# An attention kernel fused with an MLP: a different mask for the first chunks, ScalarE copies, reordered loads, one more crossbar transpose and a split last output block

## The chip, the cores and the metric

The kernel runs on one core of one Trainium2 chip. The metric is device time in microseconds (us) of one execution, lower is better. The span that a profile shows is some 1.8 us shorter than the time of the same execution (218.6 against 220.45 us for the kernel before).

TensorE does the matmuls (PE in the profile, PEld its weight loads), VectorE (DVE) and ScalarE (ACT) the elementwise work, GpSimd (POOL) some elementwise work and the issuing of the loads, SyncE (SP) the issuing of the stores and of the transposing DMAs.

## The reference, cut to what matters

Lightning attention (linear attention with a decay per head) feeds an MLP with an ELU.

```python
# q, k, v: [B=4, H=8, S=768, D=64]; lam: [8]; w_in: [512, 2048]; w_out: [2048, 512]
for b in range(nb):                      # blocks of 64 rows; the kernel uses chunks of 128
    intra = (qb @ kb.T) * Dmask          # Dmask[i, j] = lam ** (i - j) for i >= j, else 0
    intra = intra @ vb
    inter = (qb * lam_pow) @ kv_state    # lam_pow[i] = lam ** (i + 1)
    out[:, :, sl] = intra + inter
    kv_state = lam ** block * kv_state + (kb * rev_pow).T @ vb
x = out.transpose(0, 2, 1, 3).reshape(B * S, H * D)    # 3072 tokens x 512
h = x @ w_in
g = where(h > 0, h, exp(min(h, 0)) - 1)
return g @ w_out
```

## The kernel before

A chunk is 128 rows of one batch element with all eight heads; there are 24, numbered g = 4c + b (c is the place in the sequence, b the batch element). Chunks 0 to 3 have no state behind them. Four chunks make a token block of the MLP, so there are six blocks. Block 0's first matmul (h = x @ w_in, 16 steps of 128 columns) is called phase A here, and its second (g @ w_out) phase B. From block 1 on the two matmuls of neighbouring blocks are interleaved, and attention chunks are woven in between. A pair of chunks has a "visit" of three parts: transposes and the decayed keys `kd`; scores `psS` and their mask; then output `psO`, state update `psU` and the copy into the MLP's input `xt`.

The decay lam^(i−j) is factored: the mask holds only the part of j (with the causal zeros), and the part of i is multiplied in by VectorE when `psO` goes to `xt`.

```python
LOADS = [(0,1,'q'), (0,1,'k'), (0,1,'v'), ..., (3,1,'k'), ('wi',0), (2,1,'v'), ('wi',1), (3,1,'v'),
         ('wi',2), ('wi',3), ('wi',4), ('wi',5), ('kd',0), ('wi',6), ('kd',2), ('wo',0), (4,2), ...]
# every load is issued by POOL in this order; ('kd', g) is a multiply on POOL between the issues

nc.scalar.activation(dn[:], loglam[:], AF.Exp, scale=pos[:, 0:1])
for hh in range(2):                                   # the mask of all chunks, once, on VectorE
    nc.vector.tensor_tensor(out=mask[:, hh], in0=causT..., in1=dn..., op=ALU.mult)
zero_states(nc.vector)                                # four memsets
# ... (cut)
def att_X(g, n, parts=1):                             # psO -> xt, with the part of i
    nc.vector.tensor_tensor(out=xt[t][...], in0=po[...], in1=qs[...], op=ALU.mult)
# ... (cut)
def mm1(t, n, alt=False):                             # one step of the first MLP matmul
    ...
    nc.scalar.activation(e[:], pH[:], AF.Exp)
    if alt:                                           # steps 3, 5, 7 of block 0: VectorE does the rest
        return e, None, pH
    nc.scalar.activation(r[:], pH[:], AF.Relu)
    return e, r, pH

def elu(t, n, e, r, pH):                              # g = min(e - 1, r): two inputs in SBUF
    nc.vector.scalar_tensor_tensor(out=gt[t][:, n, :], in0=e[:], scalar=-1.0, in1=r[:],
                                   op0=ALU.add, op1=ALU.min)
# ... (cut)  mm2, the last output block:
    nc.vector.tensor_copy(o[:, 0:hw], pm[:, 0:hw]);  nc.sync.dma_start(...)
    nc.scalar.copy(o[:, hw:], pm[:, hw:]);           nc.scalar.dma_start(...)
# ... (cut)  the start: warm-up matmuls between the parts, W[i] of them each
W = [5, 2, 3, 0, 1, 0, 0, 1, 1, 0, 0]
# ... (cut)  pairs whose q and k are transposed by a DMA, and the step that issues it
XT = {12: (1, 10), 14: (2, 2), 16: (2, 10), 18: (3, 2), 20: (3, 10), 22: (4, 2)}
visits: 4 at A11, A13, A15;  6 at B6, B9, B12;  8 at (1,0), (1,2), (1,5);  10 at (1,8), (1,10), (1,13) ...
```

Of the kernel before, what the change touches and what calls it, by code (L numbers as in the profile page):

```python
# [15 lines left out]
def kernel(  # L16
# [93 lines left out]
        [cpool.tile([128, 2, HP, 128], FP16, name=f"st{j}_{i}") for i in range(2)]  # L110
        for j in range(B // 2)
    ]
    def zero_states(e):
        for j in range(B // 2):
            for i in range(2):
                e.memset(st[j][i][:], 0.0)

    LOADS = [(0, 1, 'q'), (0, 1, 'k'), (0, 1, 'v'), (1, 1, 'q'), (1, 1, 'k'), (1, 1, 'v'), (2, 1, 'q'), (2, 1, 'k'), (3, 1, 'q'), (3, 1, 'k'), ('wi', 0), (2, 1, 'v'), ('wi', 1), (3, 1, 'v'), ('wi', 2), ('wi', 3), ('wi', 4), ('wi', 5), ('kd', 0), ('wi', 6), ('kd', 2), ('wo', 0), (4, 2), ('wo', 1), (6, 2), ('wo', 2), ('wo', 3), (8, 2), (10, 2), (12, 2), (14, 2), (16, 2), (18, 2), (20, 2), (22, 2)]

    def run_loads(items):  # L120
        for it in items:
# [18 lines left out]
    ident16 = cpool.tile([128, 128], FP16, name="ident16")  # L140
    causT = cpool.tile([128, 128], FP32, name="causT")
    rel = cpool.tile([128, 128], FP32, name="rel")
    nc.vector.tensor_copy(rel[:], rel_i[:])
    nc.vector.tensor_copy(pos[:, 0:1], rel[:, 0:1])
    nc.vector.tensor_scalar(
        out=ident16[:], in0=rel[:], scalar1=0.0, scalar2=None, op0=ALU.is_equal
    )
    nc.vector.tensor_scalar_add(pos[:, 1:2], pos[:, 0:1], float(L))
    nc.vector.tensor_scalar(
        out=causT[:], in0=rel[:], scalar1=0.0, scalar2=None, op0=ALU.is_ge  # L150
    )
    nc.vector.tensor_scalar(
        out=row[:], in0=rel[:], scalar1=pos[:, 0:1], scalar2=None, op0=ALU.subtract
    )

    dn = cpool.tile([128, H], FP32, name="dn")
    nc.scalar.activation(dn[:], loglam[:], AF.Exp, scale=pos[:, 0:1])
    mask = cpool.tile([128, 2, HP, 128], FP32, name="mask")
    for hh in range(2):
        nc.vector.tensor_tensor(  # L160
            out=mask[:, hh],
            in0=causT[:].unsqueeze(1).broadcast_to([128, HP, 128]),
            in1=dn[:, hh::2].unsqueeze(2).broadcast_to([128, HP, 128]),
            op=ALU.mult,
        )

    zero_states(nc.vector)
    ks = cpool.tile([128, H], FP32, name="ks")
    up_p = cpool.tile([128, HP], FP32, name="up_p")
    qs = cpool.tile([128, HP, 128], FP32, name="qs")  # L170
    loglam_p = cpool.tile([128, HP], FP32, name="loglam_p")

    def late_consts():
        for hh in range(2):
            r = slice(hh * 64, (hh + 1) * 64)
            nc.scalar.copy(loglam_p[r, :], loglam[r, hh::2])
        for hp in range(HP):
            nc.scalar.activation(
                qs[:, hp, :], row[:], AF.Exp, scale=loglam_p[:, hp : hp + 1]
            )  # L180
        nc.scalar.activation(ks[:], loglam[:], AF.Exp, scale=pos[:, 1:2])
        nc.scalar.activation(up_p[:], loglam_p[:], AF.Exp, scale=float(L))



# [72 lines left out]
    def att_mask(g, parts=1):  # L258
        P = asb.tile([128, 2, HP, 128], FP16, tag="P", name=f"P{g}", bufs=3)
        s = pS.pop(g)  # L260
        w = HP // parts
        for i in range(parts):
            c = slice(i * w, (i + 1) * w)
            nc.vector.tensor_tensor(  # L264
                out=P[:, :, c], in0=s[:, :, c], in1=mask[:, :, c], op=ALU.mult
            )
        Pt[g] = P

# [24 lines left out]
    def att_X(g, n, parts=1):  # L293
        t, i = where[g]
        if i == 0:
            xt[t] = asb.tile([128, HP, TS[t] * L], FP16, tag="xt", name=f"xt{t}")
        po = pS.pop(("O", g))
        w = HP // parts
        for j in range(parts):
            c = slice(j * w, (j + 1) * w)  # L300
            nc.vector.tensor_tensor(  # L301
                out=xt[t][:, c, i * L : (i + n) * L].rearrange("p h (n l) -> p n h l", n=n),
                in0=po[:, :, c],
                in1=qs[:, c].unsqueeze(1).broadcast_to([128, n, w, 128]),
                op=ALU.mult,
            )
# [68 lines left out]
            )  # L375

    def mm1(t, n, alt=False):
        MT = TS[t] * L
        if (t, n) not in pH_of:
            mm1_mm(t, n, 0, MT, "M" if t == 0 and n % 2 == 1 and n < 8 else "H")  # L380
        pH = pH_of.pop((t, n))
        e = msb.tile([128, MT], FP32, tag="e", bufs=3, name=f"e{t}_{n}")
        nc.scalar.activation(e[:], pH[:], AF.Exp)  # L383
        if alt:
            return e, None, pH
        r = msb.tile([128, MT], FP16, tag="r", bufs=3, name=f"r{t}_{n}")
        nc.scalar.activation(r[:], pH[:], AF.Relu)  # L387
        return e, r, pH

    def elu(t, n, e, r, pH):  # L390
        if r is None:
            m = msb.tile([128, TS[t] * L], FP16, tag="r", bufs=3, name=f"m{t}_{n}")
            nc.vector.tensor_scalar(
                out=m[:], in0=e[:], scalar1=-1.0, scalar2=0.0, op0=ALU.add, op1=ALU.min
            )
            nc.vector.tensor_tensor(out=gt[t][:, n, :], in0=m[:], in1=pH[:], op=ALU.max)  # L396
            return
        nc.vector.scalar_tensor_tensor(  # L398
            out=gt[t][:, n, :], in0=e[:], scalar=-1.0, in1=r[:], op0=ALU.add, op1=ALU.min
        )  # L400

    def mm2(t, i, n, tag="M"):
        if n == 0:
            psM[t, i] = ps.tile([128, DM], FP32, tag=tag, bufs=2, name=f"psM{t}_{i}")
        pm = psM[t, i]
        nc.tensor.matmul(  # L406
            pm[:], lhsT=gt[t][:, n, i * L : (i + 1) * L],
            rhs=wo_t[wo_at[n][0]][:, wo_at[n][1], :], start=(n == 0), stop=(n == NF - 1),
        )
        if n < NF - 1:  # L410
            return
        c, b = divmod(T0[t] + i, B)
        t0 = b * S + c * L
        o = msb.tile([128, DM], FP32, tag="osb", bufs=3, name=f"osb{t}_{i}")
        last = T0[t] + i == NG - 1
        if last:
            hw = DM // 2
            nc.vector.tensor_copy(o[:, 0:hw], pm[:, 0:hw])
            nc.sync.dma_start(out=out[t0 : t0 + L, 0:hw], in_=o[:, 0:hw])
            nc.scalar.copy(o[:, hw:], pm[:, hw:])  # L420
            nc.scalar.dma_start(out=out[t0 : t0 + L, hw:], in_=o[:, hw:])
        else:
            if i % 2:
                nc.vector.tensor_copy(o[:], pm[:])  # L424
            else:
                nc.scalar.copy(o[:], pm[:])  # L426
            nc.sync.dma_start(out=out[t0 : t0 + L, :], in_=o[:])
        psM.pop((t, i))
# [23 lines left out]
    def op_T(c, w):  # L452
        att_T(c, 1, w, "H")

    def op_Te(c, w):
        att_Te(c, 1, w, "a")

    W = [5, 2, 3, 0, 1, 0, 0, 1, 1, 0, 0]
    warm(W[0])
    op_T(0, "q")  # L460
    op_Te(0, "q")
    warm(W[1])
    op_T(0, "k")
    op_Te(0, "k")
    late_consts()
    warm(W[2])
    att_S(0)
    att_mask(0, 2)
# [6 lines left out]
    att_O(0, 1, "M")  # L475
    att_X(0, 1)
    warm(W[5])
    op_T(2, "q")
    op_Te(2, "q")
    att_S(1)  # L480
    att_mask(1, 2)
    warm(W[6])
    op_T(2, "k")
    op_Te(2, "k")
    op_T(3, "q")
    op_Te(3, "q")
    warm(W[7])
    att_S(2)
    att_mask(2, 2)
    op_T(3, "k")  # L490
    op_Te(3, "k")
    att_O(1, 1, "M")
    att_X(1, 1)
    warm(W[8])
    att_S(3)
    att_O(2, 1, "M")
    att_X(2, 1)
    att_mask(3, 2)
    warm(W[9])
    for n in range(1):  # L500
        mm1_mm(0, n, 0, 3 * L, "HM"[n % 2])
    att_O(3, 1)
    att_X(3, 1, 2)
    warm(W[10])
    for n in range(1, 3):
        mm1_mm(0, n, 0, 3 * L, "HM"[n % 2])
    for n in range(3):
        mm1_mm(0, n, 3 * L, 4 * L)

    run_loads(LOADS[17:27])  # L510
    for s, g in zip([], (0, 2)):
        at(s, att_kd, g, 2)
# [3 lines left out]
        at(s, att_st, g)  # L516
        at(s, att_tmp, g + B)

    XT = {12: (1, 10), 14: (2, 2), 16: (2, 10), 18: (3, 2), 20: (3, 10), 22: (4, 2)}

    def visit(g, s0, s1, s2):
        if g in XT:
            at(XT[g], att_xT, g)
        else:
            at(s0, att_T, g, 2, "q")
            at(s0, att_T, g, 2, "k")
            at(s0, att_Te, g, 2, "q", "a")
            at(s0, att_Te, g, 2, "k", "a")
        at(s0, att_kd, g, 2, "p" if g in () else "v")
        at(s1, att_S, g)  # L530
        at(s1, att_S, g + 1)
        at(s1, att_mask, g)
        at(s1, att_mask, g + 1)
        at(s2, att_O, g, 2)
        at(s2, att_U, g)
        at(s2, att_X, g, 2)
        at(s2, att_st, g)
        at(s2, att_tmp, g + B)

    for g, vs in [(4, (('A', 11), ('A', 13), ('A', 15))), (6, (('B', 6), ('B', 9), ('B', 12))), (8, ((1, 0), (1, 2), (1, 5))), (10, ((1, 8), (1, 10), (1, 13))), (12, ((2, 0), (2, 2), (2, 5))), (14, ((2, 8), (2, 10), (2, 13))), (16, ((3, 0), (3, 2), (3, 5))), (18, ((3, 8), (3, 10), (3, 13))), (20, ((4, 0), (4, 2), (4, 5))), (22, ((4, 8), (4, 10), (4, 13)))]:  # L540
        visit(g, *vs)
    for s, a, b in [(('A', 14), 27, 28), (('A', 15), 28, 29), (('B', 11), 29, 30), (('B', 13), 30, 31), ((1, 1), 31, 32), ((1, 5), 32, 33), ((1, 9), 33, 34), ((1, 13), 34, 35)]:
        at(s, run_loads, LOADS[a:b])
# [43 lines left out]
```

## Time and profile before

| | before |
|---|---|
| time, median of 3 runs | 220.01 us (219.97 to 220.41) |
| span of the profiled run | 218.6 us |
| first Exp of the MLP | 20.05 us |
| end of the last ReLU of phase A | 40.81 us |
| first matmul of block 1 (called b1 below) | 53.49 us |
| first run of four `psM` matmuls in block 2 (called b2 below) | 79.01 us |
| end of the last matmul | 214.31 us |

These landmarks cut the span into start, phase A, phase B, block 1, the dense rest and the tail.

The first view is the slice table of the kernel before: 40 equal slices of 5.5 us, each digit the busy share in tenths; PEclk is the granted clock of TensorE in tenths.

```profile
PE   5979789899998999999999999999999999999992
DVE  2775879997799999897887786776666544534000
ACT  5643899332978876456466566456456566674110
PEclk9999999999999999999999999999999999999999
DMA  6999999999999999999143052061011011110221
```

TensorE's row stays at nine from the fourteenth slice (71 us) on, and from 80 us the next view has TensorE busy without a gap, at full clock throughout. Before that no engine is full all the time. The DMA row is near full for the first 19 slices, about 100 us.

The next view gives the busy time of the engines in stretches; the columns are the window, its length, busy us (and instructions) of PE, PEld, DVE, ACT and POOL, then granted clock, DMA share and GB/s.

```profile
10.00:15.00 5.00, 3.90 (x55) 2.39 (x53) 3.35 (x6) 3.22 (x6) 5.00 (x8) 1.00 2.21 155
15.00:20.00 5.00, 4.07 (x44) 2.28 (x44) 3.65 (x7) 0.13 (x1) 4.92 (x6) 1.00 1.57 177
...
60.00:70.00 10.00, 9.52 (x97) 5.05 (x95) 9.94 (x12) 7.62 (x14) 7.66 (x7) 1.00 2.08 174
...
80.00:100.00 20.00, 20.00 (x162) 9.71 (x160) 18.44 (x22) 11.86 (x23) 9.13 (x8) 1.00 2.62 164
```

ScalarE is idle from 15 to 20 us while POOL is full: a start that waits for loads. From 60 to 70 us VectorE has 0.06 us to spare, so there it sets the pace. From 80 us on TensorE does.

The chain of waits of the kernel before (start, length, what) says the same. These are four of its pieces.

```profile
12.60 4.99 DMA vn<-in_v_dram
...
59.09 2.35 DVE P L264 x2
...
65.72 1.56 DVE g L398
...
69.37 0.76 issue
```

The start ends with the landing of the last v; block 1 runs through VectorE.

Last, some single instructions from the timeline before (start, length, engine, line, operation, operands, and in brackets how long the engine had been idle and what ended that).

```profile
19.31 1.92 POOL L239 TENSOR_TENSOR kd<-kn,ks 128x1024 f16<-128x1024 f16 x1
20.05 0.60 ACT L383 ACTIVATE e<-psH 128x512 f32<-128x512 f32 x1 [4.92 <-PE psH L372]
21.17 0.69 DVE L398 SCALAR_TENSOR_TENSOR g<-e,r 128x512 f16<-128x512 f32 x1 [2.12 <-ACT r L387]
...
70.32 0.62 PE L252 MATMUL psS<-qT,kT 64*128 64x128 f16 x16 [0.80 <-ACT kT L218]
...
214.40 0.42 DVE L418 COPY osb<-psM 128x256 f32<-128x256 f32 x1 [6.27 <-PE psM L406]
214.86 0.37 ACT L420 COPY osb<-psM 128x256 f32<-128x256 f32 x1 [3.38 <-DVE osb L418]
```

The first Exp comes after 4.92 us in which ScalarE had nothing to do. TensorE waits 0.80 us for the transposed k of chunk 10. At the end ScalarE's copy waits for VectorE's.

### The profile page before, as it was taken

The page shows a single profiled execution, that of the slowest core. Times are in us where ns is not written, and L with a number is a line of the kernel's source. Part 1 is how long each engine was busy: PE and PEld are TensorE (multiplying, and loading weights), DVE is VectorE, ACT ScalarE, POOL GpSimd, SP SyncE. Part 2 cuts the span into 40 slices and gives each one's busy share as a digit, 9 for nine tenths or more (in the row PEclk, how much of TensorE's full clock was granted, in tenths as well). Part 3 has the DMA queues.
Part 4 walks back from the last instruction along what each step waited for, and adds up shares of the span by engine and source line. Part 5 has one row for each costly group of instructions (what it writes and reads, how often), then busy time and mean ns, then how long its engine had stood idle before and what let it go on. Part 6 is the DMA issues. An engine that isn't in the chain of part 4 may idle for free.

```text
span 218.6 us, 3968 instructions
## 1 busy us (share of the span) xinstructions
PE 204.8 (94%) x1593; PEld 100.3 (46%) x1593; DVE 150.3 (69%) x190; ACT 126.8 (58%) x234; POOL 79.2 (36%) x76
## 2 busy tenths in 40 slices
PE   5979789899998999999999999999999999999992
PEld 1444334455554544544544544545445444444440
DVE  2775879997799999897887786776666544534000
ACT  5643899332978876456466566456456566674110
POOL 8999979699958478210300000000000000000000
PEclk9999999999999999999999999999999999999999
DMA  6999999999999999999143052061011011110221
GB/s 42 144 158 190 206 163 182 183 176 157 200 184 154 157 149 167 144 166 184 39 96 97 3 116 76 2 138 58 0 48 51 0 48 48 49 51 0 96 96 49
DMA packets 96643, 23.33 MB, mean 107 GB/s; under 512 B 88816, under 2 KB 93680, under 8 KB 96624
## 3 DMA queue, kind: packets, MB, share of 16 engines
q0 software_dynamic: 80208, 13.63, 89.2%
q1 hardware_dynamic: 16272, 9.31, 18.1%
q8 instruction: 12, 0.20, 0.4%
q10 hardware_dynamic: 144, 0.13, 0.2%
q14 instruction: 7, 0.06, 0.1%
HBM read 27.27 MB, written 6.29 MB: 153 GB/s over the span
## 4 chain that ended last, share of the span: by engine, by line
PE 71%; DVE 13%; POOL 5%; ACT 5%; issue 2%; DMA 2%; DVEq 0%; POOLq 0%; ACTq 0%
PE psM L406 34%; PE psH L372 30%; DVE g L398 5%; DVE P L264 3%; PE psO L277 2%; DMA vn<-in_v_dram 2%; ACT e L383 2%; ACT r L387 2%; DVE kd L239 2%; POOL qn L72 2%; POOL kn L72 2%; PE psO L285 2%; PE psS L252 2%; POOL vn L72 1%; DVE st L355 1%
## 5 line engine op out<-in xcount | busy, mean ns | idle before, releaser
L372 PE MATMUL psH<-xt,wi 128*128 128x512 f16 (+2 forms) x396 | 98.0, 372 | 2.8 <-DVE g L396 1.1
L406 PE MATMUL psM<-wo,g 128*128 128x512 f16 x384 | 97.6, 380 | 0.0
L398 DVE SCALAR_TENSOR_TENSOR g<-e,r 128x512 f16<-128x512 f32 x93 | 71.3, 780 | 37.5 <-ACT r L387 37.3
L383 ACT ACTIVATE e<-psH 128x512 f32<-128x512 f32 x96 | 57.6, 604 | 59.3 <-PE psH L372 56.8
L372 PEld LDWEIGHTS <-wi 128*128 128x128 f16 x396 | 37.8, 98 | 47.6 <-issue 5.2
L387 ACT ACTIVATE r<-psH 128x512 f16<-128x512 f32 x93 | 55.7, 599 | 0.0
L406 PEld LDWEIGHTS <-g 128*128 128x128 f16 x384 | 36.2, 98 | 41.9
L264 DVE TENSOR_TENSOR P<-psS,mask 128x1024 f16<-128x1024 f32 (+1 forms) x28 | 28.7, 1066 | 3.1 <-PE psS L252 3.0
L336 POOL TENSOR_TENSOR tmp<-st,up_p 64x512 f32<-64x512 f16 x16 | 21.6, 1347 | 21.2 <-DVE st L355 20.3
L301 DVE TENSOR_TENSOR xt<-psO,qs 128x1024 f16<-128x1024 f32 (+2 forms) x15 | 15.0, 1008 | 7.2 <-PE psO L285 6.3
L72 POOL DMA_DIRECT2D vn<-in_v_dram x14 | 15.4, 1102 | 4.2 <-issue 4.2
L426 ACT COPY osb<-psM 128x512 f32<-128x512 f32 x12 | 7.0, 591 | 16.1 <-PE psM L406 16.1
L72 POOL DMA_DIRECT2D qn<-in_q_dram x14 | 15.7, 1124 | 1.4 <-issue 1.4
L72 POOL DMA_DIRECT2D kn<-in_k_dram x14 | 15.3, 1091 | 1.9 <-issue 1.9
L277 PE MATMUL psO<-P,vn 128*64 128x128 f16 x192 | 12.4, 223 | 1.0 <-DVE P L264 0.8
L277 PEld LDWEIGHTS <-vn 128*64 128x64 f16 x192 | 10.0, 110 | 6.3 <-issue 5.5
L424 DVE COPY osb<-psM 128x512 f32<-128x512 f32 x11 | 7.6, 689 | 5.9 <-PE psM L406 5.8
L239 DVE TENSOR_TENSOR kd<-kn,ks 128x1024 f16<-128x1024 f16 x8 | 11.5, 1443 | 0.0
L355 DVE TENSOR_TENSOR st<-tmp,psU 64x512 f16<-64x512 f32 x16 | 10.9, 680 | 0.2
L285 PE MATMUL psO<-qT,st 128*64 128x128 f16 x160 | 10.3, 219 | 0.0
L285 PEld LDWEIGHTS <-st 128*64 128x64 f16 x160 | 9.0, 110 | 0.0
L252 PE MATMUL psS<-qT,kT 64*128 64x128 f16 x192 | 8.0, 221 | 0.9 <-ACT kT L218 0.8
(44 smaller groups left out, 80.4 us busy)
## 6 DMA issues: line engine op xcount, KB each, us to landing
out_dram<-osb SPq DMA_DIRECT2D x23, 256.0 KB, 2.2
qn<-in_q_dram POOLq DMA_DIRECT2D x10, 256.0 KB, 12.6
kn<-in_k_dram POOLq DMA_DIRECT2D x10, 256.0 KB, 14.2
vn<-in_v_dram POOLq DMA_DIRECT2D x10, 256.0 KB, 13.7
wo<-in_moe_w_out_dram POOLq DMA_DIRECT2D x4, 512.0 KB, 13.2
wi<-in_moe_w_in_dram POOLq DMA_DIRECT2D x2, 512.0 KB, 8.4
wi<-in_moe_w_in_dram POOLq DMA_DIRECT2D x3, 256.0 KB, 6.1
qn<-in_q_dram POOLq DMA_DIRECT2D x4, 128.0 KB, 4.4
```

Of the source, the lines that this page charges most:

```text
L72: nc.gpsimd.dma_start(out=dst, in_=src[b : b + n, :, rows].rearrange("b h p d -> p (b h) d"))
L239: e.tensor_tensor(out=kd[:].rearrange("p (n h) d -> p n h d", n=n), in0=heads(kn, g, n).rearrange("p (n h) d -> p n h d", n=n), in1=ks_b, ...
L264: nc.vector.tensor_tensor(out=P[:, :, c], in0=s[:, :, c], in1=mask[:, :, c], op=ALU.mult)
L277: nc.tensor.matmul(po[r, i, hp, :], lhsT=v_of(g + i, 2 * hp + hh), rhs=P[:, hh, hp, :], start=True, stop=(c == 0), skip_group_check=True,)
L285: nc.tensor.matmul(po[r, i, hp, :], lhsT=st[(g + i) % B // 2][c % 2][:, (g + i) % 2, hp, r], rhs=qT[g + i][:, hp, :], start=False, stop=Tr ...
L301: nc.vector.tensor_tensor(out=xt[t][:, c, i * L : (i + n) * L].rearrange("p h (n l) -> p n h l", n=n), in0=po[:, :, c], in1=qs[:, c].unsqu ...
L336: e.tensor_tensor(out=tmp[r], in0=old[r, :, :, r], in1=up_p[r].unsqueeze(1).unsqueeze(3).broadcast_to([64, 2, HP, 64]), op=ALU.mult,)
L372: nc.tensor.matmul(pH[:, lo:hi], lhsT=wi[:, kk, j * 128 : (j + 1) * 128], rhs=xt[t][:, kk, lo:hi], start=(kk == 0), stop=(kk == HP - 1),)
L383: nc.scalar.activation(e[:], pH[:], AF.Exp)
L387: nc.scalar.activation(r[:], pH[:], AF.Relu)
L398: nc.vector.scalar_tensor_tensor(out=gt[t][:, n, :], in0=e[:], scalar=-1.0, in1=r[:], op0=ALU.add, op1=ALU.min)
L406: nc.tensor.matmul(pm[:], lhsT=gt[t][:, n, i * L : (i + 1) * L], rhs=wo_t[wo_at[n][0]][:, wo_at[n][1], :], start=(n == 0), stop=(n == NF - 1),
```

## The change

The intent: (1) for chunks 0 to 3, which have no state, the mask takes the full decay, so the way from `psO` to `xt` is a plain copy that the idle ScalarE can do; the factored mask that all later chunks need is built at step A1, over the first one. (2) The last two v loads go ahead of the first weights. (3) The first visits come one step later in phase A and B (the last part of visit 4 two steps, from A15 to B1). (4) Pair 10 (chunks 10 and 11) is transposed by DMA through the crossbar instead of by TensorE and ScalarE. (5) The last output block is computed in two halves of the columns, so that less is left to copy at the end.

```diff
-    LOADS = [..., (3, 1, 'k'), ('wi', 0), (2, 1, 'v'), ('wi', 1), (3, 1, 'v'), ('wi', 2), ...]
+    LOADS = [..., (3, 1, 'k'), (2, 1, 'v'), (3, 1, 'v'), ('wi', 0), ('wi', 1), ('wi', 2), ...]
+    nc.vector.tensor_scalar_max(lag[:], rel[:], 0.0)
+    def build_mask0(hh):
+        for h in range(hh, H, 2):
+            nc.scalar.activation(mask[:, hh, h // 2, :], lag[:], AF.Exp, scale=loglam[:, h : h + 1])
+        nc.vector.tensor_tensor(out=mask[:, hh], in0=mask[:, hh], in1=causT..., op=ALU.mult)
+    def late_mask():        # the mask as it was before, by VectorE
 ...
 def att_X(g, n, parts=1):
+            if g < B:
+                if j == 1:
+                    nc.vector.tensor_copy(dst, po[:, :, c])
+                else:
+                    nc.scalar.copy(out=dst, in_=po[:, :, c])
+                continue
 ...
+    def mm2_last(t, i):     # 2 x 16 matmuls of half the width
+        for x in range(2):
+            ...
+            # half 0: one copy by VectorE; half 1: a quarter by VectorE, a quarter by ScalarE
 ...
-    W = [5, 2, 3, 0, 1, 0, 0, 1, 1, 0, 0]
+    W = [5, 2, 3, 0, 1, 0, 0, 0, 0, 0, 0]
 ...                        # only step 0 of phase A runs ahead (before: steps 0 to 2)
+    at(('A', 1), late_mask)
+    at(('A', 4), zero_state, 0, 0)
+    at(('A', 4), zero_state, 1, 0)
 ...
-    XT = {12: (1, 10), ...}
+    XT = {10: (1, 2), 12: (1, 10), ...}
 ...
-    (4, (('A', 11), ('A', 13), ('A', 15))), (6, (('B', 6), ('B', 9), ('B', 12)))
+    (4, (('A', 12), ('A', 14), ('B', 1))), (6, (('B', 7), ('B', 10), ('B', 13)))
```

Not in the list above, but in the diff: two warm-up matmuls of the start are dropped, and only step 0 of phase A runs ahead. Left out: the reordering of the start around the copies, and code for blocks of two chunks that nothing uses.

## The prediction

> **What bounds the kernel now.** The slice table shows two regimes. From about 80 us the TensorE slices are full and the chain of waits is an unbroken alternation of psH and psM matmuls (0.86 us per four) to 214.3 us; the stretches 80–100, 100–120 … show TensorE 20.0 of 20 us. The diff touches nothing there. What can change is the start (0–20 us), the first two blocks (20–80 us) and the tail (214.3–218.6 us). In the timeline the first matmul of the MLP starts at 16.75, the first Exp at 20.05; block 1 starts at 53.3. Stretches: 20–40 us ScalarE 18.0 of 20; 40–50 VectorE 9.9 of 10; 60–80 VectorE 19.6 of 20. Dense matmuls take 0.216 us each (psM x68 in 14.7), so the real TensorE work of 18–79 us is (my estimate from the counts and dense pieces) about 53 of 61 us. The whole pool to win from is thus about 7 us there, plus the start.
>
> **Removed or moved earlier.**
> - The chain of waits in the start runs through thirteen POOL issues to the last v load (issued 12.60, landing +4.99), then psO of chunk 3 at 17.62. Two weight issues (0.75, 0.64) move behind it: it lands about 1.4 us sooner. Also only n=0 is run ahead; before, its last quarter stood behind n=2, whose weights were waited for at 18.96.
> - Exp no longer waits for that. But ScalarE becomes the start's own limit: from 4.83 us it has eight mask Exps (0.32 each), eight transposed copies (0.59), qs and small ones (2.2), dn (0.3), and 3.5 xt copies (0.59), about 12 us. Estimate: first Exp at 18.5–19.
> - Chunks 10/11 through the crossbar: TensorE loses 16 transposes (pieces of 0.45 dense, 0.9 us), ScalarE two copies (1.02 + 1.04), and the 0.80 us TensorE idle before psS at 70.3 (released by kT) should go. VectorE is full there, so I count 1.0–1.2 us. The operands land 5.2 us after issue; needed 8 steps later.
> - Tail: the last copies were serial (VectorE 0.42, then ScalarE 0.37, which waited for it). PSUM — Partial Sum Buffer, "PSUM bank collisions raise a hardware error", in the Trainium skill says two engines must not use one bank at once; the wait on record agrees. A quarter each is left: estimate 0.29 + 0.27, saving about 0.3 us. I take 32 half-width matmuls to cost what 16 did.
>
> **Added.** VectorE gets the final mask (2 x 0.65) and two memsets (2 x 0.53) at steps 1 and 4 of block 0: 2.35 us where it idled about 1.85 us in 20–30. VectorE works without pause from 33.8 to 50, so I count 0.5–1.0 paid back. Chunk 4's visit a step later avoids the wait for its k (0.75 us idle).
>
> **Sum:** –1.3 start, –1.1 crossbar, –0.3 tail, –0.4 fewer load waits, +0.8 VectorE: –2.3 us. Predicted 217.7 us, range 215.2 to 219.6; faster by over 2% 0.12, same 0.86, slower 0.02.
>
> **What would show it.** Right: first Exp near 18.7; block 1's first psH near 52.5; no TensorE psT after about 60 us and no kT-released idle near 69; psM/psH alternation unchanged; last copy to end 0.3 us shorter. Wrong: first Exp no earlier (ScalarE start overrun); ScalarE Exp waiting on g in steps 3–8 (VectorE backlog); psS of chunk 10 waiting for a DMA transpose.
>
> **What would make it wrong.** VectorE backlog eating the whole gain; or the reverse, block 0 being paced by ScalarE so that all of the start plus load waits carries through (then about –4).

## The result, and the profile after

| | before | after |
|---|---|---|
| time, median of 4 runs each | 219.99 us (219.78 to 220.41) | 218.85 us (218.68 to 219.27) |
| ratio | | 0.9949 (95% interval 0.9928 to 0.9969): the same within 2% |
| first Exp | 20.05 | 20.19 |
| end of the last ReLU of phase A | 40.81 | 40.33 |
| b1 | 53.49 | 53.39 |
| `psS` of chunk 10 | 70.32 | 68.94 |
| b2 | 79.01 | 77.42 |
| end of the last matmul | 214.31 | 212.77 |

Ratios here and below are the mean time of one kernel's fast runs over that of the other's fast runs of the same rounds, so not quite the ratio of the medians. The gain is 1.1 us where 2.3 was predicted.

The first thing that was not foreseen is the granted clock. The clock's row of the slice table of the kernel after, then the two stretches of its start (columns as before):

```profile
PEclk9976999999999999999999999999999999999999
```

```profile
10.00:15.00 5.00, 3.77 (x53) 2.40 (x50) 3.01 (x6) 3.43 (x8) 5.00 (x8) 0.83 2.34 154
15.00:20.00 5.00, 3.93 (x36) 2.27 (x34) 2.66 (x5) 2.03 (x4) 4.92 (x6) 0.50 1.44 176
```

TensorE ran at half clock from 13.3 to 20.1 us, where before the clock was 1.00. The instructions of the timeline after that answer to those shown of before:

```profile
19.22 1.92 POOL L250 TENSOR_TENSOR kd<-kn,ks 128x1024 f16<-128x1024 f16 x1
20.19 0.60 ACT L416 ACTIVATE e<-psH 128x512 f32<-128x512 f32 x1 [1.45 <-PE psH L390]
21.31 0.69 DVE L433 SCALAR_TENSOR_TENSOR g<-e,r 128x512 f16<-128x512 f32 x1 [1.57 <-ACT r L420]
...
68.94 0.62 PE L263 MATMUL psS<-qT,kT 64*128 64x128 f16 x16 [0.37 <-DMA kT<-kn]
...
212.80 0.29 DVE L456 COPY osl<-psM 128x128 f32<-128x128 f32 x1 [1.26 <-PE psM L446]
213.17 0.27 ACT L458 COPY osl<-psM 128x128 f32<-128x128 f32 x1 [3.28 <-DVE osl L456]
```

The first Exp is no earlier, because its matmuls ran at half clock. The tail is as predicted: of the last output only two quarter copies, one after the other, are left. The chain of waits after, between 52 and 72 us, has lost its many pieces on VectorE and ScalarE for one long one:

```profile
57.57 11.32 DMA kT<-kn
...
68.94 0.62 PE psS L263 x16
```

The crossbar transpose that was issued at 57.57 took 11.32 us to land, and TensorE waited the last 0.37 us of it. That is a new wait, but shorter than the 0.80 us that it replaced.

By the landmarks, this pair of profiles gained 0.1 us up to b1, 1.5 us between b1 and b2, nothing in the dense rest (135.3 us from b2 to the last matmul's end in both), and 0.25 us in the tail (end of the last matmul to the last store's issue: 214.31 to 215.26 before, 212.77 to 213.47 after). So the question is: where did the gain of the start go? The obvious answer, the half clock, turns out to be incomplete.

### The profile page after: what moved, and what is told of

Its sections match the earlier page's. It is cut to its first block, busy times and chain, and to the rows that moved or that the text cites. A ratio compares the mean times of both kernels' runs of the same rounds, so it can differ in the third digit from the quotient of the medians.

```text
span 216.9 us, 3963 instructions
## 1 busy us (share of the span) xinstructions
PE 204.9 (94%) x1583; PEld 101.4 (47%) x1583; DVE 146.0 (67%) x190; ACT 128.9 (59%) x244; POOL 78.9 (36%) x76
## 4 chain that ended last, share of the span: by engine, by line
PE 77%; DMA 7%; DVE 6%; ACT 3%; POOL 3%; issue 1%; POOLq 0%; SPq 0%; ACTq 0%
PE psM L471 34%; PE psH L390 31%; DMA kT<-kn 5%; PE psO L289 3%; PE psS L263 3%; DMA qn<-in_q_dram 2%; DVE g L433 2%; PE psO L297 2%; DVE P L275 2%; PE psM L446 2%; POOL qn L72 1%; POOL kn L72 1%; PE psU L337 1%; ACT r L420 1%; DVE kd L250 1%
## 5 line engine op out<-in xcount | busy, mean ns | idle before, releaser
L471 PE MATMUL psM<-wo,g 128*128 128x512 f16 x368 | 94.5, 380 | 0.4 <-DVE g L431 0.4
L433 DVE SCALAR_TENSOR_TENSOR g<-e,r 128x512 f16<-128x512 f32 x93 | 67.5, 743 | 37.2 <-ACT r L420 36.9
L471 PEld LDWEIGHTS <-g 128*128 128x128 f16 x368 | 34.5, 98 | 40.3 <-DMA wo<-in_moe_w_out_dram 0.4
L320 DVE TENSOR_TENSOR xt<-psO,qs 128x1024 f16<-128x1024 f32 x10 | 12.2, 1220 | 5.9 <-PE psO L297 5.9
L289 PE MATMUL psO<-P,vn 128*64 128x128 f16 x192 | 13.1, 233 | 1.8 <-DVE P L275 1.8
L250 DVE TENSOR_TENSOR kd<-kn,ks 128x1024 f16<-128x1024 f16 x8 | 12.1, 1507 | 0.1
L263 PEld LDWEIGHTS <-kT 64*128 64x128 f16 x192 | 5.7, 98 | 7.8 <-ACT kT L229 4.2
```

The lines of the kernel that those rows point to most:

```text
L250: e.tensor_tensor(out=kd[:].rearrange("p (n h) d -> p n h d", n=n), in0=heads(kn, g, n).rearrange("p (n h) d -> p n h d", n=n), in1=ks_b, ...
L263: nc.tensor.matmul(s[:, hh, hp, :], lhsT=kT[g][r, hp, :], rhs=qT[g][r, hp, :], start=True, stop=True,)
L289: nc.tensor.matmul(po[r, i, hp, :], lhsT=v_of(g + i, 2 * hp + hh), rhs=P[:, hh, hp, :], start=True, stop=(c == 0), skip_group_check=True,)
L433: nc.vector.scalar_tensor_tensor(out=g, in0=e[:], scalar=-1.0, in1=r[:], op0=ALU.add, op1=ALU.min)
L471: nc.tensor.matmul(pm[:], lhsT=gt[t][:, n, i * L : (i + 1) * L], rhs=wo_t[wo_at[n][0]][:, wo_at[n][1], :], start=(n == 0), stop=(n == NF - 1),
```

## The experiments

Theory 1 ("clock"): the start's gain is real and was eaten by the half clock that came with the two removed warm-up matmuls.

Theory 2 ("VectorE backlog"): the deferred mask and the two memsets, 2.3 us of VectorE work in phase A, eat it.

Theory 3 ("floor"): something that the change doesn't move, POOL's chain of issues or the landings behind it, sets when block 1 can start, and an earlier start only waits longer.

Names beginning with a_ are made from the kernel after, with b_ from the kernel before, with c_ have another schedule as well. Each was timed in five rounds (6 runs) beside 11 runs of the kernel before on the same chip; single fast runs of one kernel in a call spread by 0.8 to 3.2 us, so differences under half a microsecond need several calls or the landmarks. The medians below are over all runs, the ratios over the fast ones.

| label | median us | before | ratio (95%) |
|---|---|---|---|
| b_again (unchanged before) | 219.96 | 220.55 | 0.9982 (0.9938 to 1.0026) |
| a_again (unchanged after) | 219.03 | 220.62 | 0.9950 (0.9912 to 0.9989) |
| a_third (unchanged after) | 219.27 | 220.55 | 0.9951 (0.9919 to 0.9984) |
| a_only_start | 220.36 | 220.55 | 0.9995 (0.9958 to 1.0032) |
| a_pe10 | 218.96 | 220.63 | 0.9957 (0.9917 to 0.9996) |
| a_pe10_b | 220.08 | 220.55 | 0.9983 (0.9953 to 1.0013) |
| b_x10 | 219.09 | 220.62 | 0.9960 (0.9917 to 1.0003) |
| a_warm | 218.44 | 220.63 | 0.9931 (0.9894 to 0.9968) |
| a_warm_b | 218.64 | 220.33 | 0.9941 (0.9897 to 0.9985) |
| a_relief | 219.10 | 220.63 | 0.9960 (0.9918 to 1.0001) |
| a_both | 218.56 | 220.63 | 0.9932 (0.9886 to 0.9978) |
| b_drop6 (wrong result) | 219.47 | 220.62 | 0.9972 (0.9933 to 1.0010) |
| a_drop6 (wrong result) | 217.74 | 220.62 | 0.9892 (0.9854 to 0.9930) |
| a_relief_drop6 (wrong result) | 217.93 | 220.26 | 0.9910 (0.9868 to 0.9952) |
| a_both_drop6 (wrong result) | 217.42 | 220.26 | 0.9886 (0.9841 to 0.9931) |
| c_late | 223.27 | 220.26 | 1.0153 (1.0104 to 1.0203) |
| c_late_all | 224.23 | 220.26 | 1.0190 (1.0148 to 1.0232) |
| c_swap | 219.01 | 220.33 | 0.9964 (0.9922 to 1.0006) |

The landmarks of their profiles, one execution each, in us. The column "first g" has start and length of VectorE's first `g`. "Exp 9" is the Exp of step 9 of phase A.

| kernel | first Exp | first g | Exp 9 | end of A's last ReLU | b1 | b1 to b2 |
|---|---|---|---|---|---|---|
| before | 20.05 | 21.17, 0.69 | 29.87 | 40.81 | 53.49 | 25.52 |
| b_again | 20.79 | 21.90, 0.69 | 30.98 | 41.52 | 54.09 | 24.69 |
| b_x10 | 20.52 | 21.64, 0.69 | 29.98 | 41.16 | 53.90 | 24.11 |
| after | 20.19 | 21.31, 0.69 | 30.11 | 40.33 | 53.39 | 24.03 |
| a_again | 19.64 | 20.75, 0.97 | 31.10 | 41.33 | 53.85 | 24.00 |
| a_third | 18.56 | 19.68, 2.02 | 29.93 | 40.76 | 53.52 | 23.96 |
| a_only_start | 19.23 | 20.34, 1.36 | 29.93 | 40.15 | 53.28 | 24.72 |
| a_pe10 | 19.25 | 20.36, 1.35 | 29.94 | 40.29 | 53.48 | 25.50 |
| a_pe10_b | 18.44 | 19.55, 2.15 | 29.93 | 40.77 | 53.82 | 25.52 |
| a_warm | 19.61 | 20.73, 0.99 | 30.33 | 41.16 | 54.20 | 23.92 |
| a_warm_b | 19.21 | 20.33, 1.37 | 29.93 | 40.20 | 53.39 | 24.10 |
| a_relief | 20.57 | 21.69, 0.69 | 30.17 | 40.78 | 53.80 | 24.24 |
| c_swap | 19.30 | 20.42, 1.28 | 29.92 | 40.14 | 53.78 | 24.17 |
| b_drop6 | 20.91 | 22.03, 0.69 | 30.37 | 40.91 | 52.83 | 24.94 |
| a_drop6 | 19.16 | 20.28, 0.69 | 29.27 | 39.50 | 52.31 | 23.84 |
| a_relief_drop6 | 19.43 | 20.55, 0.69 | 30.40 | 40.62 | 53.08 | 23.99 |
| a_both_drop6 | 19.37 | 20.49, 0.69 | 30.12 | 40.35 | 52.74 | 24.26 |

### The same kernels again: b_again, a_again, a_third

No edit.

> The kernel before as a kernel of this call, for a second profile of it. First Exp 20.0-20.9, block 1's start 53.4-54.2, block 1's to block 2's start 25.5, ratio to itself 1.000 within 0.3%.

> The changed kernel as it is, again, beside the kernels of this call, because single runs of one call differed by up to 2.5 us. 1.0 to 1.3 us under the kernel before of the same call. Block 1's start at 53.0-54.2 and 23.9-24.3 us from block 1's start to block 2's.

> The changed kernel again, beside its own version without the crossbar entry for chunk 10 in the same call. As before: 1.1 us under the kernel before.

The times confirm the result: the fast runs of the kernel before have a mean of 220.15 us (58 runs, standard error 0.11) and the kernel after 219.19 us (12 runs, 0.17), so the gain is 1.0 us. That b_again differs from its own kernel by 0.6 us in the median of one call shows how little one call settles.

The profile of a_third is a lucky find. In that execution the clock stayed at 1.00 through the start, and the first Exp came at 18.56 us, as predicted. Yet b1 came at 53.52 us, no earlier than before. This refutes theory 1 as the whole cause: 1.5 us of start were won and lost again with no half clock at all. (It is one execution; the clocks of all runs, below under a_warm, say the same.) The timeline of a_third shows where it went first.

```profile
18.56 0.60 ACT L416 ACTIVATE e<-psH 128x512 f32<-128x512 f32 x1 [0.82 <-PE psH L390]
19.22 1.92 POOL L250 TENSOR_TENSOR kd<-kn,ks 128x1024 f16<-128x1024 f16 x1
19.68 2.02 DVE L433 SCALAR_TENSOR_TENSOR g<-e,r 128x512 f16<-128x512 f32 x1 [0.94 <-ACT r L420]
21.62 1.28 DVE L177 TENSOR_TENSOR mask<-causT,dn 128x512 f32<-128x512 f32 x2
23.60 0.60 ACT L416 ACTIVATE e<-psH 128x512 f32<-128x512 f32 x1 [1.08 <-DVE g L433]
25.22 1.03 DVE L114 MEMSET st<- 128x512 uint32 x2
```

The first `g` began at 19.68, but took 2.02 us instead of 0.69. It ended at 21.70, 0.56 us after POOL's second `kd` (19.22 + 1.92 = 21.14). In the table, whenever the first `g` began before about 21.1 us in a kernel whose w_in loads are all in place (POOL's second `kd` ends at 21.14 to 21.17 in all of them, in c_swap too, where another load's issue stands before it), its start and its length add up to 21.70 to 21.72 us, wherever it began: 19.55 + 2.15, 19.68 + 2.02, 20.33 + 1.37, 20.34 + 1.36, 20.36 + 1.35, 20.42 + 1.28, 20.73 + 0.99, 20.75 + 0.97. So VectorE could do nothing with an earlier start. The Trainium skill has this rule: "SBUF — State Buffer", section "Who interferes with whom", says that a VectorE instruction with two inputs in SBUF contends with a GpSimd instruction that reads SBUF, because both need the one shared read port. `g` has two such inputs (e and r), `kd` reads kn and ks. This agrees, and the counterexample is there too: at 16.57 in the profile of the kernel after, two `P` operations with one input in PSUM took 1.29 us beside POOL's first `kd` (16.55, 1.90), which is 0.65 us each, their usual length.

After that the kernels run in step. ScalarE waits for the late `g` (1.08 us at 23.60, another 0.73 at 26.88), and Exp 9 comes at 29.92 to 29.94 in six of the profiles, whose first Exp lies anywhere from 18.44 to 19.30. The kernel before has it at 29.87. VectorE's deferred mask and memsets (1.28 and 1.03 us) lie in this same stretch.

### The start alone: a_only_start

```diff
-    XT = {10: (1, 2), 12: (1, 10), ...}
+    XT = {12: (1, 10), ...}
 (and the last output block as it was before)
```

> The changed kernel without the crossbar entry for chunk 10 and with the old last block: the start, the moved visits and the deferred mask alone. If the start gives nothing (block 1's start 53.4-54.2 in every profile so far): the time of the kernel before, within 0.4 us. If it gives what I predicted (1.3 + 0.4 - 0.8): 0.9 us under it.

The time is that of the kernel before, 220.36 against 220.55 us. The interval still allows a gain of 0.9 us, so the landmarks have to narrow it: the mean b1 of the three profiles with the old start (before, b_again, b_x10) is 53.83 us, and of the six with the new start and nothing else done to it (after, a_again, a_third, a_only_start, a_pe10, a_pe10_b) 53.56 us. The start, with the load order, the moved visits and the VectorE work, is thus worth about 0.3 us, where 0.9 had been predicted for these terms together (1.3 + 0.4 − 0.8). The values of each group spread over 0.6 us, so 0.3 is not clear of zero.

The same means for the end of the last ReLU of phase A are 41.16 and 40.61 us, a gain of 0.55; half of it is gone by b1. The third part of visit 4 moved from A15 to B1, so phase B got that work; where b1 is really decided comes out under a_drop6.

### The crossbar: b_x10, a_pe10, a_pe10_b

```diff
 b_x10 (on the kernel before):          -    XT = {12: (1, 10), ...}
                                        +    XT = {10: (1, 2), 12: (1, 10), ...}
 a_pe10, a_pe10_b (on the kernel after): the reverse
```

> The kernel before with only chunk 10 moved to the crossbar. Crossbar theory: block 1's start to block 2's shrinks from 25.5 to 24.0-24.3 us, the whole by 1.2-1.5 us. Rival (the crossbar needs the earlier loads that the moved visits bring, since before chunk 10's loads are issued only at 46.5-50 us): psS of chunk 10 waits for the transposed k by 1 us or more, and the whole gains under 0.6 us.

> The changed kernel with chunk 10 transposed on TensorE again (only the crossbar entry for 10 undone). My prediction's term was 1.1 us; the two profiles differ by 1.5 us between block 1's start and block 2's start. Theory: 1.1 to 1.6 us slower than the changed kernel, so about 219.9-220.5, back at the time of the kernel before. Rival (the gain between blocks 1 and 2 comes from the earlier loads and moved visits, not from the crossbar): under 0.5 us slower.

> Repeat of the changed kernel with chunk 10 on TensorE, now in one call with the changed kernel. In the profiles every kernel with the crossbar entry took 23.9-24.2 us from block 1's start to block 2's and every one without 25.5 us, yet the timed medians of the two calls were equal. If the profiles are right: 1.0-1.5 us slower than the changed kernel of this call. If the timed medians are right: within 0.4 us of it, and the profiled run shows the start of block 1 earlier by as much as blocks 1 to 2 take longer.

From b1 to b2 the five profiles without this transpose (before, b_again, a_only_start, a_pe10, a_pe10_b) take 25.19 us in the mean, and the four with it (b_x10, after, a_again, a_third) 24.03 us. That is 1.16 us, and 1.1 had been predicted. b_x10 alone has nearly the whole gain of the change in its time (ratio 0.996, with an interval that just reaches 1). Taking it out of the change cost 0.7 us in the mean in a_pe10_b and nothing in a_pe10, compared with no run of the kernel after; pooled it is 0.36 us with a standard error of 0.25, well under the landmark's 1.16. I take the landmark to be the better witness, since the noise of the start doesn't enter it: each of the four values with the transpose (23.96 to 24.11) lies below each of the five without (24.69 to 25.52). Why the times show less is not known.

The profile of a_pe10_b has another start at full clock, and repeats what a_third showed, with the first Exp at 18.44:

```profile
19.55 2.15 DVE L433 SCALAR_TENSOR_TENSOR g<-e,r 128x512 f16<-128x512 f32 x1 [0.94 <-ACT r L420]
21.63 1.28 DVE L177 TENSOR_TENSOR mask<-causT,dn 128x512 f32<-128x512 f32 x2
```

### The clock: a_warm, a_warm_b

```diff
-    W = [5, 2, 3, 0, 1, 0, 0, 0, 0, 0, 0]
+    W = [5, 2, 3, 0, 1, 0, 0, 1, 1, 0, 0]
```

> The changed kernel with the two warm-up matmuls of the start put back (W[7] and W[8] from 0 to 1, as before). Clock theory (the start's gain was lost because TensorE's granted clock fell to 0.50 between 13.6 and 20.1 us): clock 1.00 in 10-20 us, first Exp at about 19.0 instead of 20.19, first psH of block 1 at about 52.3 instead of 53.4, time about 1.0 us under the changed kernel's 218.85, so 217.8. VectorE theory (its 2.35 us of deferred mask and memsets fill block 0, so the start doesn't matter): first Exp moves as above, but block 1 begins at 53.0-53.4 and the time stays at 218.5-218.9.

> Repeat of the changed kernel with the two warm-up matmuls. If the clock matters: 218.3-218.7 and 0.5-0.7 us under the changed kernel's 219.2. If the first call was luck: 219.0-219.4.

With the two warm-up matmuls back, the means together are 218.60 us (12 runs, standard error 0.10), 0.6 us under the kernel after. Its medians are 2.2 and 1.7 us under the kernel before, and under each of the three medians of the kernel after (218.85, 219.03, 219.27). They were run at other times. So it is the best correct version that I can name, though its lead on the kernel after is only 0.6 us. Why it leads is not shown. Its profiles still have a stretch of half clock of some 3.4 us, from about 18 us on, and b1 in them (54.20 and 53.39) is no earlier than without. What the profiles do show is that the half clock comes and goes between executions of one kernel: in the start, 3.41 or 6.83 us of it in most profiles with the new start, none in a_third, a_pe10_b, c_swap, c_late and c_late_all, and none in any profile with the old start.

Every run's mean clock, profiled or not, tells what the clock costs here. One stretch of 3.41 us at half clock lowers the mean over 217 us by 0.008. Of the 16 runs of the kernel after, eight have a mean clock of 0.992 or less; their mean time is 219.21 us, that of the other eight 219.04: a difference of 0.17 us with a standard error of 0.28. Of the 12 runs with the warm-ups six have such a clock, and both halves have a mean of 218.60 us. So the two warm-up matmuls did not keep the clock up more often, and a low clock costs these kernels nothing that can be seen. (Of the kernel before, eight of 58 fast runs have such a clock, and they are 0.76 us slower, standard error 0.23; where in those runs it fell is not on record.)

The Trainium skill, "TensorE: Matmul & The Clock Gate", section "What's actually happening", puts the half clock down to at least one idle window of about 3.4 us. The lengths seen here, 3.41 and 6.83 us, are one and two such windows. But TensorE was not idle for such a window before it: in the 3.4 us before the drop in the profile of the kernel after, no gap was over 0.56 us, and TensorE was busy for 2.17 of the 3.4 us up to 13.3. So this trace shows the clock halved after partly busy time. In c_late and c_late_all (below) it halved for 3.41 us from 46.64 and 46.78 us on, after TensorE had waited 3.71 and 4.15 us: there the rule fits.

### VectorE's deferred work: a_relief, a_both

The final mask gets a tile of its own and is built right after the first chunk's mask, and the two memsets go ahead of phase A. `row` now shares `rel`'s tile.

```diff
     att_S(0)
     att_mask(0, 2)
+    late_mask()                     # writes mask2
 ...
-                in1=mask[:, :, c], op=ALU.mult,
+                in1=(mask if g < B else mask2)[:, :, c], op=ALU.mult,
 ...
-    at(('A', 1), late_mask)
-    at(('A', 4), zero_state, 0, 0)
-    at(('A', 4), zero_state, 1, 0)
+    (the two memsets behind att_mask(1, 2) and att_mask(2, 2))
```

a_both has this and the warm-ups.

> The changed kernel with VectorE's deferred work taken out of block 0: the final mask goes into a tile of its own during the start, both memsets too, in VectorE's idle gaps. No warm-up matmul put back. Clock theory: first Exp stays at about 20.2 and the time at 218.5-218.9. VectorE theory: Exp waits for g in 23-28 us (0.9 us) vanish, block 1 begins 0.5 to 1.5 us earlier than 53.4, time 217.4-218.3.

> Both edits together. If both theories hold in part: first Exp about 19.0, no Exp wait for g, block 1 begins at 51.3-52.3, time 216.8-217.8. If each alone gives nothing and both together give over 1 us, either of the two was enough to hold block 0 back. If even both give under 0.4 us, something else (weight landings, or POOL's slowing of VectorE after 32 us) paces block 0, and both theories fall.

a_relief has the mean time of the kernel after (219.23 against 219.19 us), and a_both that of a_warm (218.61 against 218.60 us, its five fast runs). So theory 2 doesn't hold as the whole cause either: take the backlog away, and nothing is won. The reservation is that the profile of a_relief fell at half clock up to about 20 us, with the first Exp at 20.57, so no profile shows an early start without the backlog. In it the `g` of the first steps waited 0.29 us each for ScalarE's `r`, which means that VectorE had time to spare.

The profiled execution of a_both took 730.21 us (span 728.4). No other run of any kernel was near that. It is unexplained.

### The last w_in load left out: b_drop6, a_drop6, a_relief_drop6, a_both_drop6

The last w_in load, 512 KB, is not issued, and steps 12 to 15 take the tile before it. The result is wrong (relative error 0.705).

```diff
             if it[0] == "wi":
-                emit_wi(it[1])
+                if it[1] != 6:
+                    emit_wi(it[1])
 ...
+    for j in range(4):
+        wi_at[12 + j] = (5, j)
```

> Wrong result on purpose: the kernel before without the load of the last four 128-column groups of w_in (512 KB; their matmuls read the group before). It takes about 3 us out of the load queue ahead of w_out's first part and of chunk 4's k. Load theory (block 0 is paced by landings): first Exp unchanged at 20.05, block 1's start 0.5-2 us earlier than 53.5, whole 0.5-2 us faster. VectorE/ScalarE theory (block 0 is paced by the two engines): under 0.3 us faster.

> Wrong result on purpose: the same load left out of the changed kernel. Load theory: TensorE's wait for w_out near 30 us and for chunk 4's k near 34 us are gone, block 1's start moves from 53.4 to 51.5-52.9, and the whole gains 0.5-2 us over the changed kernel of the same call. VectorE/ScalarE theory: under 0.3 us.

> Wrong result on purpose: the changed kernel without the last w_in load and with VectorE's deferred work moved into the start. One floor (landings only): the time of the kernel with the load left out, 1.3 us under the changed kernel, about 217.9. Two floors in series (landings and VectorE's backlog): 2.0-3.0 us under the changed kernel, about 216.5, with no Exp wait for g and step 8's Exp under 29 us.

> Wrong result on purpose: the same with the two warm-up matmuls back. If the clock matters once both floors are lifted: another 0.5-1.0 us. If not: within 0.3 us of the one without them.

The edit had a side effect. Without the issue of that load POOL ran its two `kd` back to back. The timeline of a_drop6:

```profile
16.58 3.76 POOL L254 TENSOR_TENSOR kd<-kn,ks 128x1024 f16<-128x1024 f16 x2
20.28 0.69 DVE L437 SCALAR_TENSOR_TENSOR g<-e,r 128x512 f16<-128x512 f32 x1 [1.57 <-ACT r L424]
20.89 1.29 DVE L181 TENSOR_TENSOR mask<-causT,dn 128x512 f32<-128x512 f32 x2
24.49 1.02 DVE L117 MEMSET st<- 128x512 uint32 x2
```

POOL's reads are over at 20.34, the first `g` takes its 0.69 us, and mask and memsets come 0.73 us earlier than in a_third, though the first Exp was later (19.16). Exp 9 came at 29.27, the earliest of all. This supports the clash of `kd` and `g` from the other side: the point at which VectorE's chain starts follows the end of POOL's `kd`.

But it is not all. In the four kernels without the load, b1 follows Exp 9 by 22.5 to 23.0 us (a mean of 22.7); in the thirteen others by 22.8 to 23.9 (a mean of 23.5). So some 0.8 us are won after Exp 9 as well, and in b_drop6 and a_relief_drop6, whose Exp 9 is late (30.37 and 30.40), that is all there is. The two groups of intervals overlap, but b1 itself doesn't: 52.31 to 53.08 without the load (mean 52.74), 53.28 to 54.20 with it (mean 53.70). This is theory 3: a second floor behind the first. Two more signs of it are a_again and b_again. Their Exp 9 is about a microsecond late (31.10 and 30.98), and b1 only 0.3 to 0.4 us behind the other profiles with the same start (53.85 and 54.09). In mean times, leaving the load out is worth 1.3 us on the kernel after (217.86 against 219.19) and 0.6 us on the kernel before (219.54 against 220.15).

The experiment alone can't tell whether the second floor is the landings (less traffic) or POOL's time (its later issues come 0.8 us earlier). The traces tell more. Behind its load issues POOL runs four multiplies `tmp` (the old state times its decay, two inputs in SBUF), and beside them VectorE runs `kd` and two `g` of chunk 4's visit. These are lines of the timelines of the kernel before and of a_third:

```profile
32.30 5.94 POOL L336 TENSOR_TENSOR tmp<-st,up_p 64x512 f32<-64x512 f16 x4
35.82 2.97 DVE L398 SCALAR_TENSOR_TENSOR g<-e,r 128x512 f16<-128x512 f32 x2
38.71 2.34 DVE L264 TENSOR_TENSOR P<-psS,mask 128x1024 f16<-128x1024 f32 x2
53.49 1.03 PE L372 MATMUL psH<-xt,wi 128*128 128x512 f16 x4
...
33.11 6.09 POOL L354 TENSOR_TENSOR tmp<-st,up_p 64x512 f32<-64x512 f16 x4
36.78 2.97 DVE L433 SCALAR_TENSOR_TENSOR g<-e,r 128x512 f16<-128x512 f32 x2
39.67 2.34 DVE L275 TENSOR_TENSOR P<-psS,mask 128x1024 f16<-128x1024 f32 x2
53.52 1.03 PE L390 MATMUL psH<-xt,wi 128*128 128x512 f16 x4
```

The two `g` take 2.97 us, where two that run undisturbed take 1.28, and end 0.55 us after the last `tmp` (32.30 + 5.94 = 38.24, and 39.20). By the same rule this is the clash of `kd` and the first `g` once more. `P` of chunk 4 stands behind them on VectorE; TensorE had finished its scores 1.7 and 1.9 us before. In all thirteen profiles of the table with the load in place a `g` ends 0.54 or 0.55 us after the last `tmp`, and `P` follows at once or after one more `g`. And b1 follows the start of that `P` at a fixed distance: 14.78 us in the three with the old start, 13.84 or 13.85 in the nine with the new one, 13.25 in c_swap. So in these profiles the second floor is where POOL's `tmp` end. Without the load they end at 36.51 to 37.39 us instead of 38.24 to 39.88. The clearest pair is the kernel after and a_drop6: from the end of `tmp` to b1 it is 14.92 us in both (38.47 to 53.39, 37.39 to 52.31), so b1 came earlier by just the 1.08 us by which `tmp` ended earlier.

This also splits the 0.3 us of the start. The moved visit makes the way from `P` to b1 0.93 us shorter (14.78 against 13.85), but `P` itself starts 0.66 us later (means of the same three and six profiles: 39.05 and 39.71). The difference is the 0.27 us by which b1 moved. No run moved `tmp` alone, so this rests on the traces and on that one pair. What makes the `tmp` start when they do is open too: they stand behind the last w_out issue, which itself waited 1.17 us in the kernel before and 1.15 in a_third. So landings may still be behind it.

That a_relief_drop6 (218.02 us) and a_both_drop6 (217.63) are no faster than a_drop6 (217.86) beyond the noise says once more that the deferred VectorE work is not the limit.

### Other schedules of phase A: c_late, c_late_all, c_swap

c_late moves visit 4 later still (A14, B0, B4) and spreads the first w_out matmuls differently, to be out of the way of the loads of chunk 4 and w_out; c_late_all adds the warm-ups and the relief. c_swap keeps the warm-ups and issues the first w_out load before the last w_in load, with visit 4 at A13, A15 and B2.

```diff
 c_late:  -    (4, (('A', 12), ('A', 14), ('B', 1))), (6, (('B', 7), ('B', 10), ('B', 13)))
          +    (4, (('A', 14), ('B', 0), ('B', 4))), (6, (('B', 6), ('B', 9), ('B', 13)))
 c_swap:  -    ('wi', 6), ('kd', 2), ('wo', 0), (4, 2)
          +    ('wo', 0), ('kd', 2), ('wi', 6), (4, 2)
          -    (4, (('A', 12), ('A', 14), ('B', 1)))
          +    (4, (('A', 13), ('A', 15), ('B', 2)))
 (in both, the w_out matmuls of phase A and B are dealt out anew)
```

> Correct kernel: the changed kernel with chunk 4's visit two steps later (A14, B0, B4) and w_out's first matmuls one step later, so that both landings have more time; the matmuls of the B steps are spread around it. VectorE's deferred work stays. Landing theory: the waits for w_out and chunk 4's k go, block 1 starts 0.3-1.0 us earlier than 53.6. If VectorE's backlog is the second floor: no gain, within 0.4 us of the changed kernel.

> Correct kernel: the late visit with VectorE's deferred work in the start and the warm-up matmuls back. Two floors: block 1 starts at 51.5-52.8, whole 217.0-218.2, under both kernels. One floor only or PE-bound B steps: within 0.4 us of the changed kernel.

> Correct kernel: the changed kernel with the warm-up matmuls, w_out's first load ahead of w_in's last, chunk 4's visit one step later (A13, A15, B2) and six pairs of w_out's matmuls moved to where their weights have landed. Load theory: TensorE's waits for w_out near 30 us and for chunk 4's k near 34 us vanish or shrink under 0.4 us, block 1 starts at 52.4-53.2, whole 217.8-218.5. If the landings aren't what paces block 0: 218.5-219.2 as the changed kernel with warm-up; if moved matmuls wait for later w_out parts as in c_late: slower.

c_late and c_late_all failed: 3 and 4 us slower than the kernel before. The new order asks for later parts of w_out before they have landed. One line of c_late_all:

```profile
46.53 0.80 PE L472 MATMUL psM<-wo,g 128*128 128x512 f16 x2 [4.15 <-DMA wo<-in_moe_w_out_dram]
```

TensorE stood still for 4.15 us. This shows how near phase B is to the landings.

c_swap was the test of the waits that remain in phase A: in a_third TensorE waits for w_out at 30.19 (0.78 us before the weight load), and for chunk 4's k at 33.98 (0.33).

```profile
30.19 0.11 PEld L471 LDWEIGHTS <-g 128*128 128x128 f16 x2 [0.78 <-DMA wo<-in_moe_w_out_dram]
```

In c_swap both waits are gone. Its start was at full clock, its ScalarE is busy almost without a gap from 28.23 to 40.14, and its Exp 9 is at 29.92 again. Its first `g` in the timeline:

```profile
20.42 1.28 DVE L433 SCALAR_TENSOR_TENSOR g<-e,r 128x512 f16<-128x512 f32 x1 [0.94 <-ACT r L420]
```

b1 was at 53.78 and the time 219.09 us in the mean, 0.5 us slower than a_warm with the old order. So these two waits by themselves were not what held b1.

## Why the prediction was right or wrong

**The start (−1.3) and the load waits (−0.4): wrong.** These are the steps that failed. The prediction took a first Exp at 18.5 to 19 us to mean "block 1's first psH near 52.5". The first half came true in two executions whose clock stayed up (18.56 in a_third, 18.44 in a_pe10_b; c_swap, with the warm-ups, had 19.30). The second never did in a correct kernel: b1 lay between 53.28 and 54.20 in all of the table, and far later in c_late and c_late_all. With the VectorE term these terms had a sum of −0.9 and measured about −0.3. The prediction looked at when the start's own chain would end, and not at what else in phase A had a timetable of its own. Two things had, both on POOL. POOL's second `kd` ends at about 21.2 us in both kernels because it stands behind POOL's chain of load issues, and an earlier `g` on VectorE is held up until then: shown by the ends at 21.70 and by a_drop6. Behind it is a second floor. It moves b1 by about 1 us (53.70 to 52.74) when one 512 KB load and its issue are left out, and by thirteen traces and the pair of after and a_drop6 it is the end of POOL's four `tmp`, at 38.2 to 39.9 us, that holds VectorE's `g` and with it `P` of chunk 4 and b1. The prediction had seen that VectorE works without pause from 33.8 us on, but took its pace as given; the two `g` there take 2.97 us for 1.28. The wait for chunk 4's k did go, as the −0.4 assumed (0.75 us before, 0.16 in a_third, none in the kernel after), but with the visit a step later `P` came 0.66 us later.

**The VectorE term (+0.8): wrong in kind.** The deferred mask and memsets do sit in VectorE's chain between 21.6 and 26.2 us, and ScalarE waits for `g` there, as the prediction said it would if it went wrong. But moving them away (a_relief, a_both) won nothing, so they are not what took the gain; in the profile of a_relief, too, the last `g` before `P` ends 0.55 us after POOL's `tmp`.

**What the prediction missed altogether: the clock.** It named "first Exp no earlier" as a sign of a ScalarE overrun. It came, in the recorded profile, from TensorE at half clock. ScalarE waited for TensorE's `psH` (1.45 us). This cost up to 1.6 us at the first Exp (20.19 against 18.56) but, behind the floors, next to nothing at b1 (53.39 against 53.52).

**The crossbar (−1.1): right** in mechanism, and in size by the landmarks: 1.16 us between b1 and b2, though the pooled times show only 0.36 with a standard error of 0.25. The landing was not: the 5.2 us that the prediction took from the median of before became 11.32 us. Issuing it eight steps ahead was 0.37 us short of enough, and that wait (the third sign named under "Wrong") did come.

**The tail (−0.3): right.** From the last matmul to the last issue it takes 0.70 us instead of 0.95. The two copies are still in turn, 0.29 and 0.27 us. The trace agrees with the Trainium skill, "PSUM — Partial Sum Buffer", section "PSUM bank collisions raise a hardware error", insofar as the program keeps the two engines from the one bank: ScalarE's copy is released by VectorE's. The 32 half-width matmuls cost what 16 did (3.51 against 16 × 0.216 = 3.46 us).

**The sum.** The three measured terms, −0.3, −1.16 and −0.25, give −1.7 us, which is the difference of the two spans (218.6 and 216.9). The timed gain is 1.0 us with a standard error of 0.2 (0.11 and 0.17 combined). The difference of 0.7 us lies in which executions were profiled: the one of before took 220.45 us, 0.3 above its kernel's mean, and the one of after 218.68, 0.5 below.

**What stays open.** Whether moving `kd` and `tmp`, to another place or another engine, would let the early start through was not run. Nor is it settled what makes `tmp` start when it does, nor why two warm-up matmuls are worth 0.6 us.

## What to carry to other kernels

Before counting a chain that ends earlier as a gain, list what in the next stretch is tied to something the change doesn't move (a queue's issues, another engine's reads, the landings), and take the latest of these as the gain's limit. A landmark that is followed from stretch to stretch over several profiles separates terms of half a microsecond that medians of runs can't. And when an expected sign comes true in one execution without the gain, follow that execution's chain further. It is one execution, so check it against all the others.

## What the Trainium skill lacked or had wrong

- "TensorE: Matmul & The Clock Gate", section "What's actually happening": it gives the half clock after an idle window of about 3.4 us. Here the clock halved with no gap over 0.56 us in the 3.4 us before, with TensorE busy for 2.17 of those 3.4 us. A later section of the page does tell of short idle times between groups of matmuls that let the clock swing; how busy is busy enough is missing in both. The lengths of 3.41 and 6.83 us fit its window.
- "SBUF — State Buffer", section "Who interferes with whom": the rule is right, and it explained the main finding. The page's summary says that the instruction issued second is fully blocked until the first has ended, and here `g` took up to 2.15 us instead of 0.69 and ended 0.56 us after the GpSimd instruction; an operation with one SBUF input ran at its usual 0.65 us beside GpSimd. It lacks what a row of GpSimd instructions does: beside four `tmp` two `g` took 2.97 us instead of 1.28.
- "DMA: Bandwidth & Descriptors", section "Latency and other measured facts": it gives a bandwidth for the transposing DMA, but no time to landing beside a full load queue. Here that was 11.32 us for the transpose that mattered, against 5.2 us in the median of the kernel before.
- "DMA: Bandwidth & Descriptors", the same section: it gives a time to the first byte for GpSimd's transfers, but not how long an issue holds up the work that stands behind it on GpSimd: 0.74 to 1.35 us each here, which is what fixed the end of `kd` at 21.2 us.
- No page that I read tells how far executions of one kernel on one core differ: 0.8 to 3.2 us of 220 here within one call, and once 730 us without a cause that the records show.
